# A planner that counts the port pair of VectorE and GpSimd as a resource, in a kernel of attention and two feed-forward networks

## Chip, cores and metric

One NeuronCore of a Trainium2 chip runs the kernel; the other cores are idle. The metric is the device time of one execution in microseconds (us). The engines are TensorE (PE in the profile's rows), VectorE (DVE), ScalarE (ACT), GpSimd (POOL) and SyncE (SP), which here issues all transfers.

## What is computed

Sliding-window attention with a distance bias, for 4 batches, 8 heads, 576 positions and head dimension 64, then a network with a softmax-weighted activation and layer norm, then a gated one, all in float32:

```python
scores = scale * np.matmul(q, k.transpose(0, 1, 3, 2))
mask = (rel >= 0) & (rel < 128)
scores = np.where(mask, scores + bias[None], -1000000000.0)
attn = np.exp(scores - np.max(scores, axis=-1, keepdims=True))
attn = attn / (np.sum(attn, axis=-1, keepdims=True) + 1e-09)
x = np.matmul(attn, v)                          # then (2304, 512)

h = x @ w_in                                    # (2304, 1024)
e = np.exp(h - np.max(h, axis=-1, keepdims=True))
solu = h * e / (np.sum(e, axis=-1, keepdims=True) + 1e-09)
mu = np.mean(solu, axis=-1, keepdims=True)
var = np.mean((solu - mu) ** 2, axis=-1, keepdims=True)
x = (solu - mu) / np.sqrt(var + 1e-06) * g_ln @ w_out

g = x @ w_gate                                  # (2304, 1536)
out = g * (1.0 / (1.0 + np.exp(-g))) * (x @ w_val) @ w_out
```

The weights arrive as 64-bit floats.

## The kernel before

**Numbers in two halves.** A float32 matrix product is made of three products of a faster type (fp32r): high by low, low by high, high by high. So each operand of the two networks exists as a high half (a cast, helper `high`, L201) and a low half (a subtraction, helper `low`, L205). `decode` (L213) turns one block of 128x512 weights into such halves: a transfer of 512 KB (tile dw), one square on ScalarE (L225), five operations on VectorE over tiles da and db (L230 to L238), an addition on GpSimd or VectorE (L241, L242), for w_out a scaling (L245), then `high` and `low`. There are 8 blocks of w_in, 8 of w_out and 36 of the second network's weights. Tiles dw, da and db have two buffers each.

**Stages.** Attention runs over 20 steps (4 batches by 5 query tiles of up to 128 rows), each of four pairs of heads, 80 units in all. `score` multiplies for two pairs at a time, one PSUM bank for each pair (L339). `attend` does the rest of a unit: for each head one VectorE operation that adds the bias and takes the maximum, out of PSUM (L372), and one exponential on ScalarE with the sum of the row as accumulator output (L375); then a sum of 1e-9 and a reciprocal over the two heads' sums (L381, L382), the normalization on GpSimd, ScalarE or VectorE (L387, L389), the transposition on TensorE (L409), a copy out of PSUM (L413 to L418) and the product with the values (L441). Results become xs, the halves of the first network's input. `up` makes a tile of 128 rows of it: two banks of 512 columns (L523), their maxima (L547, L554), exponentials (L557), products (L559), a squared deviation (L565), some one-column statistics (L561 to L574), a power on GpSimd (L579) and the normalization (L581, L582). `flip` transposes (L605), `down1` multiplies by w_out, and the result goes through DRAM (yscr). The second network, `gate_val` and `down`, takes the w2 blocks two chunks at a time, in six passes over all rows. Its first weights are decoded into the memory that attention leaves.

**Eight PSUM banks** (`bank_s`) serve the scores, transposes, values, halves of `up`, `flip` and `down1`. A unit returns its scores bank after the second L372.

**The order** is made by a planner in Python, class `Emitter`. Each stage is a generator that asks for slots (buffers) and hands in operations: an engine, a cost in ns, a function, and what it depends on. An operation may have several ways, one for each engine that can do it. `Emitter.run` takes for each operation the way with the least start + cost + handicap (`BIAS`: 1600 for VectorE, 700 for ScalarE), then the engine whose operation can start first, then the lowest rank; it calls the function, which writes the instruction, and sets the engine's busy time on by the cost. The rank goes by the row tile that the work belongs to. On the chip each engine runs its instructions in the order written, and waits only for data and buffers. So the costs decide who does what and in which order, and nothing of their times is enforced.

## Time and profile before

| what | us |
|---|---|
| median of 3 runs | 885.85 (885.5 to 887.36) |
| the profiled execution | 887.44, of which 885.7 are its span |
| TensorE busy (matmul) | 825.1, 93% of the span |
| VectorE busy | 492.9, 56% |
| ScalarE busy | 372.8, 42% |
| GpSimd busy | 317.0, 36% |
| mean granted clock of TensorE | 0.973 |

One execution was profiled; all rows come from it, with times in us from its first instruction. A busy share over the whole span is a mean over stages that differ, so the rows further down go by stretches: up to 132 us the weights of the first network are decoded beside the first attention steps, until 350 us attention and the first network run together, until 440 us the second network's first weights are decoded, and from then on it runs.

### The profile page before, as it was taken

The page shows a single profiled execution, that of the slowest core. Times are in us where ns is not written, and L with a number is a line of the kernel's source. Part 1 is how long each engine was busy: PE and PEld are TensorE (multiplying, and loading weights), DVE is VectorE, ACT ScalarE, POOL GpSimd, SP SyncE. Part 2 cuts the span into 40 slices and gives each one's busy share as a digit, 9 for nine tenths or more (in the row PEclk, how much of TensorE's full clock was granted, in tenths as well). Part 3 has the DMA queues.
Part 4 walks back from the last instruction along what each step waited for, and adds up shares of the span by engine and source line. Part 5 has one row for each costly group of instructions (what it writes and reads, how often), then busy time and mean ns, then how long its engine had stood idle before and what let it go on. Part 6 is the DMA issues. An engine that isn't in the chain of part 4 may idle for free.

```text
span 885.7 us, 13165 instructions
## 1 busy us (share of the span) xinstructions
PE 825.1 (93%) x4968; PEld 677.9 (77%) x4968; DVE 492.9 (56%) x1188; ACT 372.8 (42%) x948; POOL 317.0 (36%) x274
## 2 busy tenths in 40 slices
PE   5769879999999999968799999999999999999997
PEld 3547658788888888968588888887887887888885
DVE  5988993654556445888510186258337526822222
ACT  4667885864766656444432322122122213211110
POOL 2464661322123121665731154145216414521111
PEclk9779899999999999979999999999999999999999
DMA  7543311311121102333320022012003101100112
GB/s 253 168 138 105 96 60 44 107 37 54 50 72 49 36 8 97 119 104 112 120 94 1 1 72 72 1 49 72 24 0 86 58 1 48 47 1 13 60 57 85
DMA packets 23776, 59.12 MB, mean 67 GB/s; under 512 B 2592, under 2 KB 5280, under 8 KB 23712
## 3 DMA queue, kind: packets, MB, share of 16 engines
q1 hardware_dynamic: 23712, 58.28, 20.3%
q8 instruction: 39, 0.64, 0.3%
q14 instruction: 25, 0.20, 0.1%
HBM read 48.83 MB, written 9.44 MB: 66 GB/s over the span
## 4 chain that ended last, share of the span: by engine, by line
PE 70%; DVE 17%; POOL 4%; issue 4%; ACT 4%; DMA 1%; SPq 0%; POOLq 0%; ACTq 0%; DVEq 0%
PE gv L523 28%; PE bank L523 16%; PE o L523 15%; PE bank L441 3%; PE bank L409 3%; PE bank L339 3%; DVE db L234 2%; DVE da L230 2%; DVE da L238 2%; DVE da L236 2%; POOL db L241 2%; DVE e L372 2%; DVE db L232 1%; PE bank L605 1%; ACT e L375 1%
## 5 line engine op out<-in xcount | busy, mean ns | idle before, releaser
L523 PE MATMUL gv<-y,w 128*128 128x512 f32 (+1 forms) x1392 | 316.2, 378 | 3.1 <-POOL y L208 3.1
L523 PEld LDWEIGHTS gv<-y,w 128*128 128x128 f32 x1392 | 249.0, 189 | 57.6 <-POOL y L208 3.5
L523 PE MATMUL o<-w,a 128*128 128x512 f32 x648 | 170.0, 398 | 5.2 <-ACT ys L202 2.2
L208 POOL TENSOR_TENSOR a<-sg,a 128x512 fp32r<-128x512 f32 (+1 forms) x60 | 73.9, 1232 | 237.7 <-ACT a L202 237.2
L523 PEld LDWEIGHTS o<-w,a 128*128 128x128 f32 x648 | 121.1, 190 | 34.6 <-POOL a L208 3.8
L795 DVE TENSOR_TENSOR acc<-acc,o 128x512 f32<-128x512 f32 x90 | 61.2, 684 | 119.9 <-PE o L523 119.8
L523 PE MATMUL bank<-lnT,wout 128*128 128x256 f32 x864 | 116.9, 287 | 3.0 <-ACT lnT L202 2.5
L523 PEld LDWEIGHTS bank<-lnT,wout 128*128 128x128 f32 x864 | 109.0, 191 | 8.6 <-ACT lnT L202 2.7
L523 PE MATMUL bank<-win,xs 128*128 128x512 f32 x432 | 114.9, 404 | 0.1
L202 ACT CAST a<-sg 128x512 fp32r<-128x512 f32 (+1 forms) x59 | 34.0, 577 | 181.8 <-DVE sg L769 181.8
L769 DVE TENSOR_TENSOR sg<-sg,gv 128x512 f32<-128x512 f32 (+1 forms) x58 | 37.1, 639 | 126.7 <-PE gv L523 97.2
L241 POOL TENSOR_TENSOR db<-db,da 128x512 f32<-128x512 f32 x51 | 72.0, 1413 | 96.5 <-DVE da L238 93.9
L523 PEld LDWEIGHTS bank<-win,xs 128*128 128x128 f32 x432 | 76.5, 189 | 17.1 <-issue 2.1
L389 POOL TENSOR_TENSOR e<-e,st 128x512 f32<-128x512 f32 (+2 forms) x55 | 52.2, 948 | 103.9 <-DVE st L382 41.6
L375 ACT ACTIVATE e<-e,st 128x256 f32<-128x256 f32 (+2 forms) x160 | 75.0, 471 | 28.9 <-DVE st L372 28.8
L409 PE MATMUL bank<-ident,e 128*128 128x128 f32 (+2 forms) x288 | 47.7, 292 | 24.3 <-POOL e L389 15.0
L372 DVE CUSTOM_DVE_ANT_0 e<-bank,bias 128x256 f32<-128x256 f32 (+2 forms) x160 | 54.3, 376 | 17.2 <-PE bank L339 11.7
L409 PEld LDWEIGHTS bank<-ident,e 128*128 128x128 f32 (+2 forms) x288 | 31.4, 147 | 36.3 <-POOL e L389 18.2
L441 PE MATMUL bank<-pt,v 128*64 128x128 f32 (+2 forms) x576 | 51.4, 292 | 6.2 <-ACT pt L415 5.3
L230 DVE SCALAR_TENSOR_TENSOR da<-db,dw 128x512 f32<-128x512 f32 x52 | 46.6, 897 | 18.5 <-ACT db L225 18.4
L767 ACT ACTIVATE sg<-gv 128x512 f32<-128x512 f32 (+1 forms) x58 | 32.3, 557 | 56.3 <-PE gv L523 43.5
L202 ACT CAST w<-db 128x512 fp32r<-128x512 f32 x35 | 21.7, 621 | 80.1 <-POOL db L241 80.0
(70 smaller groups left out, 906.3 us busy)
## 6 DMA issues: line engine op xcount, KB each, us to landing
dw<-w SPq DMA_DIRECT2D x36, 512.0 KB, 3.6
raw<-qk SPq DMA_DIRECT2D x38, 256.0 KB, 3.7
yscr<-ys SPq DMA_DIRECT2D x9, 512.0 KB, 2.9
ysg<-yscr SPq DMA_DIRECT2D x9, 512.0 KB, 3.3
out<-acc SPq DMA_DIRECT2D x18, 256.0 KB, 2.0
v<-v SPq DMA_DIRECT2D x16, 256.0 KB, 2.8
dw<-w_in SPq DMA_DIRECT2D x8, 512.0 KB, 4.0
dw<-w_out SPq DMA_DIRECT2D x8, 512.0 KB, 3.5
```

The costliest lines, as they stand in the source:

```text
L202: return [(ACT, t_act(n, sbuf), lambda: nc.scalar.copy(hi, src)), (DVE, t_dve(n, sbuf), lambda: nc.vector.tensor_copy(hi, src))]
L208: ways.append((POOL, t_pool(n), lambda: nc.gpsimd.tensor_sub(lo, src, hi.bitcast(F32))))
L230: x = yield (DVE, t_dve(512), lambda: nc.vector.scalar_tensor_tensor(af, bf, MIN_HIGH * MIN_HIGH, hf, ALU.is_ge, ALU.mult), [x])
L241: x = yield ([(POOL, t_pool(512), lambda: nc.gpsimd.tensor_add(bf, bf, af)), (DVE, t_dve(512), lambda: nc.vector.tensor_add(bf, bf, af))], ...
L372: d = yield (DVE, t_dve(cols), lambda j=j: nc.vector.tensor_tensor_reduce(e[0:n, j, 0:cols], sc[0:n, j * 256:j * 256 + cols], bias[0:n, 2 ...
L375: ex.append((yield (ACT, t_act(cols, True, True), lambda j=j: nc.scalar.activation(e[0:n, j, 0:cols], e[0:n, j, 0:cols], AF.Exp, bias=st[0 ...
L389: eng.tensor_tensor(e[0:n, :, 0:cols], e[0:n, :, 0:cols], st[0:n, 6:8].unsqueeze(2).to_broadcast([n, 2, cols]), ALU.mult)
L409: nc.tensor.transpose(tp[0:kp, kb, j, 0:n], e[0:n, j, x * P:x * P + kp], ident[0:n, 0:n])
L441: nc.tensor.matmul(px[j * 64:(j + 1) * 64, pr, 0:n], vt[c - 1 + kb][0:kp, h * 64:(h + 1) * 64], pt[0:kp, kb, j, 0:n], start=(kb == 1), sto ...
L523: nc.tensor.matmul(o, terms[m][0], terms[m][1], start=(m == 0), stop=(m == len(terms) - 1))
L769: x = yield (DVE, t_dve(n), lambda: nc.vector.tensor_mul(sg, sg, gv[1][0]), [x, gv[1][1]])
L795: y = yield (DVE, t_dve(512), lambda o=o, tt=tt: nc.vector.tensor_add(acc[tt], acc[tt], o), [x])
```

## The change

`Emitter` gets a third kind of busy time, "+". Engine names that end in "+" can start only when the engine and "+" are free, and set both. All of GpSimd's operations have it (`POOL` is now "POOL+"), and of VectorE's those that read SBUF alone: the five of `decode`, the addition and scaling, `high` and `low` from SBUF, and the normalizations. VectorE's operations that read PSUM, and those on one or two columns, don't.

In `attend`, the exponentials' sums go to columns 0 and 1 of the unit's own scores bank in place of the tile st in SBUF, both L372 are handed in before both exponentials, and the bank is returned after L381 and L382. In `up`, L554, L571 and L574 take their one-column operands as pointer scalars of a `tensor_scalar`. Several costs change: matmul pieces from 216 to 233 or 231 ns for each matmul of 512 columns (109 to 120 and 0.4219 n to 0.457 n for the others), statistics of one column from 70 to 205 ns, the accumulating ScalarE operations by 93 ns, L381 and L382 from 230 to 360, L581 from 456 to 334. The handicaps and ranks stay.

```diff
+    def free(self, engine):
+        at = self.busy.get(engine.rstrip("+"), 0.0)
+        return max(at, self.busy.get("+", 0.0)) if engine.endswith("+") else at
+
     def run(self):
...
             for op in self.pending:
-                t, way = min(((max(self.busy.get(w[0], 0.0), op[2]), w) for w in op[3]), key=lambda x: x[0] + x[1][1] + BIAS.get(x[1][0], 0.0))
-                best.setdefault(way[0], []).append((t, op[0], op[1], op, way))
+                t, way = min(((max(self.free(w[0]), op[2]), w) for w in op[3]),
+                             key=lambda x: x[0] + x[1][1] + BIAS.get(x[1][0].rstrip("+"), 0.0))
+                best.setdefault(way[0].rstrip("+"), []).append((t, op[0], op[1], op, way))
             first = min(min(x[0] for x in ops) for ops in best.values())
...
             fn()
-            self.busy[engine] = t + cost
+            self.busy[engine.rstrip("+")] = t + cost
+            if engine.endswith("+"):
+                self.busy["+"] = t + cost
             op[5].settle(t + cost + self.HOP + op[4])
...
     em = Emitter()
-    PE, DVE, ACT, POOL, DMA = "PE", "DVE", "ACT", "POOL", "DMA"
+    PE, DVE, ACT, POOL, DMA = "PE", "DVE", "ACT", "POOL+", "DMA"
+    DVEP, NONE = "DVE+", "POOL"
     yscr = nc.dram_tensor("yscr", [NT // 256, P, KM, 256], F32).ap()
...
         return [(ACT, t_act(n, sbuf), lambda: nc.scalar.copy(hi, src)),
-                (DVE, t_dve(n, sbuf), lambda: nc.vector.tensor_copy(hi, src))]
+                (DVEP if sbuf else DVE, t_dve(n, sbuf), lambda: nc.vector.tensor_copy(hi, src))]
 
     def low(lo, src, hi, n, sbuf=True):
-        ways = [(DVE, t_dve(n), lambda: nc.vector.tensor_sub(lo, src, hi.bitcast(F32)))]
+        ways = [(DVEP if sbuf else DVE, t_dve(n), lambda: nc.vector.tensor_sub(lo, src, hi.bitcast(F32)))]
         if sbuf:
...
         af = a.bitcast(F32)
-        x = yield (DVE, t_dve(512), lambda: nc.vector.scalar_tensor_tensor(
+        x = yield (DVEP, t_dve(512), lambda: nc.vector.scalar_tensor_tensor(
             af, bf, MIN_HIGH * MIN_HIGH, hf, ALU.is_ge, ALU.mult), [x])
-        x = yield (DVE, t_dve(512, True), lambda: nc.vector.tensor_scalar(
+        x = yield (DVEP, t_dve(512, True), lambda: nc.vector.tensor_scalar(
             b, a, 3, 0x3FFFFFF8, ALU.logical_shift_left, ALU.bitwise_and), [x])
-        x = yield (DVE, t_dve(512), lambda: nc.vector.scalar_tensor_tensor(
+        x = yield (DVEP, t_dve(512), lambda: nc.vector.scalar_tensor_tensor(
             b, a, 0xC0000000, b, ALU.bitwise_and, ALU.bitwise_or), [x])
-        x = yield (DVE, t_dve(512, True), lambda: nc.vector.tensor_scalar(
+        x = yield (DVEP, t_dve(512, True), lambda: nc.vector.tensor_scalar(
             a, b, 0xFF800000, None, ALU.bitwise_and), [x])
-        x = yield (DVE, t_dve(512), lambda: nc.vector.scalar_tensor_tensor(
+        x = yield (DVEP, t_dve(512), lambda: nc.vector.scalar_tensor_tensor(
             af, lw, 2.0 ** -52, af, ALU.mult, ALU.mult), [x])
...
         x = yield ([(POOL, t_pool(512), lambda: nc.gpsimd.tensor_add(bf, bf, af)),
-                    (DVE, t_dve(512), lambda: nc.vector.tensor_add(bf, bf, af))], [x])
+                    (DVEP, t_dve(512), lambda: nc.vector.tensor_add(bf, bf, af))], [x])
         em.give(da_s, x)
...
             x = yield ([(ACT, 93 + t_act(512), lambda: nc.scalar.activation(bf, bf, AF.Copy, scale=scale)),
-                        (DVE, 456, lambda: nc.vector.tensor_scalar_mul(bf, bf, scale))], [x])
+                        (DVEP, 456, lambda: nc.vector.tensor_scalar_mul(bf, bf, scale))], [x])
         x = yield (high(hi, bf, 512), [x])
...
         bs_ok = bias_ok[0] if t == 0 and c == 0 else bias_ok[1]
-        ex = []
+        ex, ds = [], []
         for j in range(2):
...
                 -0.125, 3.0e38, ALU.add, ALU.min, st[0:n, j:j + 1]), [x, bs_ok])
-            ex.append((yield (ACT, t_act(cols, True, True), lambda j=j: nc.scalar.activation(
+            ds.append(d)
+        for j, d in enumerate(ds):
+            ex.append((yield (ACT, 93 + t_act(cols, True, True), lambda j=j: nc.scalar.activation(
                 e[0:n, j, 0:cols], e[0:n, j, 0:cols], AF.Exp, bias=st[0:n, j:j + 1], scale=-1.0,
-                accum_out=st[0:n, 2 + j:3 + j]), [d])))
-        em.give(bank_s, d, k)
+                accum_out=sc[0:n, j:j + 1]), [d, ds[0]])))
 
         def invert():
-            nc.vector.tensor_scalar_add(st[0:n, 4:6], st[0:n, 2:4], 1e-9)
+            nc.vector.tensor_scalar_add(st[0:n, 4:6], sc[0:n, 0:2], 1e-9)
             nc.vector.reciprocal(st[0:n, 6:8], st[0:n, 4:6])
...
 
-        x = yield (DVE, 230, invert, ex)
-        x = yield ([(DVE, t_dve(2 * cols), lambda: normalize(nc.vector)),
+        x = yield (DVE, 360, invert, ex)
+        em.give(bank_s, x, k)
+        x = yield ([(DVEP, t_dve(2 * cols), lambda: normalize(nc.vector)),
                     (ACT, 2 * (93 + t_act(cols)), lambda: normalize(nc.scalar)),
...
             terms = [(xs[a][:, k], win[c][:, k, cs]) for a, c in HALVES for k in range(KM)]
-            for p in pieces(h[q], terms, 6, 216.0):
+            for p in pieces(h[q], terms, 6, 233.0):
                 x = yield p
...
         es[i] = e
-        x = yield (DVE, 70, lambda: nc.vector.tensor_tensor(mx, mx, mx2, ALU.min), tops)
+        x = yield (DVE, 205, lambda: nc.vector.tensor_scalar(mx, mx, mx2, None, ALU.min), tops)
         us = []
         for q, (a, a2) in enumerate(((sm, su), (sm2, su2))):
-            y = yield (ACT, t_act(512, False, True), lambda q=q, a=a: nc.scalar.activation(
+            y = yield (ACT, 93 + t_act(512, False, True), lambda q=q, a=a: nc.scalar.activation(
                 e[:, q], h[q], AF.Exp, bias=mx, accum_out=a), [x])
...
                 e[:, q], h[q], 1.0, e[:, q], ALU.mult, ALU.mult, accum_out=a2), [y])))
-        x = yield (DVE, 70, lambda: nc.vector.tensor_scalar(
+        x = yield (DVE, 205, lambda: nc.vector.tensor_scalar(
             nmu32, su, su2, -1.0 / (32 * DF1), ALU.add, ALU.mult), us)
...
         for q, a in enumerate((va, va2)):
-            vs.append((yield (ACT, t_act(512, True, True), lambda q=q, a=a: nc.scalar.activation(
+            vs.append((yield (ACT, 93 + t_act(512, True, True), lambda q=q, a=a: nc.scalar.activation(
                 h[q], e[:, q], AF.Square, bias=nmu32, scale=1.0 / 32, accum_out=a), [x])))
...
             nc.vector.tensor_scalar(s1, sm, sm2, 1e-9, ALU.add, ALU.add)
-            nc.vector.scalar_tensor_tensor(eps, s1, 1e-6, s1, ALU.mult, ALU.mult)
-
-        y = yield (DVE, 280, moments, [x])
-        x = yield (DVE, 70, lambda: nc.vector.scalar_tensor_tensor(var, va, va2, eps, ALU.add, ALU.add), vs + [y])
+            nc.vector.tensor_scalar(eps, s1, 1e-6, s1, ALU.mult, ALU.mult)
+
+        y = yield (DVE, 615, moments, [x])
+        x = yield (DVE, 205, lambda: nc.vector.tensor_scalar(var, va, va2, eps, ALU.add, ALU.add), vs + [y])
         em.give(h_s, x)
...
         for q in range(2):
-            last = yield ([(DVE, 456, lambda q=q: nc.vector.tensor_scalar(
+            last = yield ([(DVEP, 334, lambda q=q: nc.vector.tensor_scalar(
                 e[:, q], e[:, q], nmu, rr, ALU.add, ALU.mult)), (POOL, 754, lambda q=q: nc.gpsimd.tensor_scalar(
...
             terms = [(wout[c][:, k, cs], ln[a][:, k]) for a, c in HALVES for k in range(KF1)]
-            for p in pieces(o[:, m % 2, :], terms, 12, 109.0):
+            for p in pieces(o[:, m % 2, :], terms, 12, 120.0):
                 x = yield p
...
             yield from decode(t[0][:, cs], t[1][:, cs], w2[c, :, cs])
-            x = yield (POOL, 0.0, lambda: None)
+            x = yield (NONE, 0.0, lambda: None)
             yield x
...
             terms = [(w[b][:, s * 512 + k * P:s * 512 + (k + 1) * P], y[a][:, k]) for a, b in HALVES for k in range(KM)]
-            for p in pieces(o, terms, 6, 0.4219 * n):
+            for p in pieces(o, terms, 6, 0.457 * n):
                 x = yield p
...
             terms = [(aT[c, g][a][:, cs], wc[c][b][:, 1024:1536]) for a, b in HALVES for c in cs2]
-            for p in pieces(o, terms, 3 * CPP, 216.0):
+            for p in pieces(o, terms, 3 * CPP, 231.0):
                 x = yield p
...
```

## Rows read from the trace of the kernel before

**Rows 1.** Busy time by stretch: PE, PEld, DVE, ACT, POOL, clock, DMA share, GB/s.

```profile
22.00:132.00 110.00, 84.96 (x596) 63.19 (x597) 104.74 (x297) 82.99 (x235) 59.89 (x53) 0.86 0.36 114
132.00:350.00 218.00, 216.59 (x1836) 182.21 (x1834) 114.54 (x469) 138.48 (x432) 54.80 (x67) 1.00 0.16 51
350.00:440.00 90.00, 73.45 (x482) 67.03 (x483) 70.89 (x113) 40.51 (x76) 54.99 (x38) 0.92 0.38 123
440.00:886.00 446.00, 438.96 (x1990) 357.75 (x1988) 190.18 (x269) 101.97 (x180) 141.73 (x108) 1.00 0.13 42
```

**Rows 2.** Chain of waits, 22 to 132 us, shares by line (the view cuts it).

```profile
by line: DVE da L230 11.1%; DVE e L372 10.7%; DVE db L234 9.7%; DVE da L238 7.8%; issue 6.8%; DVE db L232 5.0%; DVE da L236 5.0%; DVE st L381 4.8%; DVE mst L547 4.0%; DVE e L559 3.7%; ACT e L375 3.6%; DVE xs L206 3.1%; PE bank L409 2.9%; DV
```

**Rows 3.** TensorE's waits, 22 to 132 us: total us, times, longest.

```profile
PE bank L409 <- POOL e L389: 14.2, 6, 5.5
```

**Rows 4.** VectorE's operations, 22 to 132 us: busy us, mean ns, idle before.

```profile
L230 DVE SCALAR_TENSOR_TENSOR da<-db,dw 128x512 f32<-128x512 f32 x14 | 14.7, 1059 | 0.0
L234 DVE SCALAR_TENSOR_TENSOR db<-da,db 128x512 uint32<-128x512 uint32 x14 | 12.3, 878 | 0.0
L238 DVE SCALAR_TENSOR_TENSOR da<-dw,da 128x512 f32<-128x512 uint32 x14 | 11.0, 789 | 0.0
L381 DVE TENSOR_SCALAR st<-st 128x2 f32<-128x2 f32 (+1 forms) x26 | 9.5, 365 | 2.8 <-ACT e L375 2.7
L236 DVE TENSOR_SCALAR da<-db 128x512 uint32<-128x512 uint32 x14 | 7.8, 557 | 0.0
L232 DVE TENSOR_SCALAR db<-da 128x512 uint32<-128x512 uint32 x14 | 6.2, 448 | 0.0
...
L554 DVE TENSOR_TENSOR mst<-mst 128x1 f32<-128x1 f32 x5 | 3.3, 667 | 0.0
L206 DVE TENSOR_TENSOR win<-db,win 128x512 fp32r<-128x512 f32 x2 | 3.2, 1582 | 0.0
...
L571 DVE SCALAR_TENSOR_TENSOR mst<-mst 128x1 f32<-128x1 f32 x4 | 1.7, 436 | 0.1
...
L569 DVE TENSOR_SCALAR mst<-mst 128x1 f32<-128x1 f32 x4 | 0.8, 201 | 0.0
```

**Rows 5.** Timeline: start us, us, operation; GpSimd beside VectorE, then VectorE alone.

```profile
29.75 1.58 POOL L241 TENSOR_TENSOR db<-db,da 128x512 f32<-128x512 f32 x1 [2.57 <-DVE da L238]
...
30.13 1.22 DVE L381 TENSOR_SCALAR st<-st 128x2 f32<-128x2 f32 x1
...
113.98 1.22 POOL L582 TENSOR_SCALAR e<-e,mst 128x512 f32<-128x512 f32 x1
114.47 0.68 DVE L547 TENSOR_REDUCE mst<-bank 128x1 f32<-128x512 f32 x1
...
51.41 0.42 DVE L232 TENSOR_SCALAR db<-da 128x512 uint32<-128x512 uint32 x1
...
74.32 0.68 DVE L234 SCALAR_TENSOR_TENSOR db<-da,db 128x512 uint32<-128x512 uint32 x1
```

**Rows 6.** Timeline of VectorE: scores of 128 columns, and one unit's scores and sum.

```profile
80.45 0.28 DVE L372 CUSTOM_DVE_ANT_0 e<-bank,bias 128x128 f32<-128x128 f32 x1
...
113.17 0.42 DVE L372 CUSTOM_DVE_ANT_0 e<-bank,bias 128x256 f32<-128x256 f32 x1
...
119.64 0.16 DVE L381 TENSOR_SCALAR st<-st 128x2 f32<-128x2 f32 x1
```

**Rows 7.** ScalarE's operations, 22 to 132 us: busy us, mean ns, idle before.

```profile
L387 ACT ACTIVATE e<-e,st 128x256 f32<-128x256 f32 (+2 forms) x20 | 8.5, 475 | 5.0 <-DVE st L382 4.8
```

**Rows 8.** Chain of waits, 350 to 440 us, shares by line (the view cuts it).

```profile
by line: PE bank L523 19.9%; POOL db L241 11.1%; PE gv L523 11.1%; issue 8.7%; DMA dw<-w 8.2%; POOL w L208 6.1%; DVE da L230 4.4%; DVE db L234 4.1%; POOL y L208 3.7%; DVE da L236 3.6%; POOL e L582 3.4%; ACT w L202 2.8%; DVE lnT L206 2.7%; D
```

**Rows 9.** Low halves, 350 to 440 us: busy us, mean ns, idle before.

```profile
L206 DVE TENSOR_TENSOR w<-db,w 128x512 fp32r<-128x512 f32 x3 | 2.1, 687 | 0.0
...
L208 POOL TENSOR_TENSOR y<-ysg,y 128x1024 fp32r<-128x1024 f32 x5 | 12.9, 2586 | 10.8 <-ACT y L202 10.8
L208 POOL TENSOR_TENSOR w<-db,w 128x512 fp32r<-128x512 f32 x9 | 12.3, 1367 | 5.1 <-ACT w L202 5.1
```

## The prediction

> **What bounds the kernel now.** A mean over the whole span says little here, so the first view is the table by stretch [rows 1]. Over its four stretches TensorE works for 84.96+216.59+73.45+438.96 = 814 of 864 us. From 132 to 350 us and from 440 us on it is full, 216.59 of 218 us and 438.96 of 446, at a granted clock of 1.00, the upper of the two levels: whatever happens on the other engines can shorten these 664 us by no more than the 8.4 us that they leave. The other two stretches are different. From 22 to 132 us TensorE works for 84.96 of 110 us at a mean clock of 0.86, and VectorE for 104.74: VectorE is the full engine. From 350 to 440 us TensorE works for 73.45 of 90 us, VectorE for 70.89 and GpSimd for 54.99. So 25 + 16.5 us of idle TensorE time, and some clock, are what the change can win.
>
> The second view, the chain of waits of the first of these stretches, says the same: the VectorE parts that its line prints add up to 11.1+10.7+9.7+7.8+5.0+5.0+4.8+4.0+3.7+3.1 = 65% [rows 2]. The third, TensorE's own waits, has another name at its head: 14.2 us, in six waits, for GpSimd's normalized exponentials, L389 [rows 3]. I keep that for a rival.
>
> Why is VectorE full? In its table of operations [rows 4] many means are far over what the operation takes elsewhere, and the timeline shows why. L381, a sum over two columns, takes 1.22 us while a GpSimd addition of 1.58 us runs [rows 5], and 0.16 us at another place [rows 6]. L547, which reads PSUM, takes 0.68 us although L582 runs on GpSimd beside it [rows 5]. So for some forms, those that read SBUF tensors alone, the two engines exclude each other, and the loser waits for the whole operation of the other.
>
> **The change, part by part.**
>
> (a) The sums of exponentials go to the scores' own PSUM bank, so L381 reads PSUM. For its 26 instances at 365 ns [rows 4] I expect 185: between the 160 of a free instance [rows 6] and L569's 201 [rows 4]. An outer bound is 280, what L372 takes for 128 columns out of PSUM [rows 6]. Saved: 26 x 0.18 = 4.7 us of VectorE; with the bounds 2.2 to 5.3. [...]
>
> (b) L554, L571 and L574 become the form with pointer scalars, which L569 has now, at 201 ns [rows 4]. L554 stands five times at 667; L571 four times at 436, and L574 as often and much alike. Saved: 5 x 0.46 + 8 x 0.23 = 4.2 us. The bound on the other side is that the new forms are stopped like the old ones: 0.
>
> (c) The rule of choice: GpSimd's operations and VectorE's SBUF forms now share one more busy time. Each GpSimd operation raises it, so a VectorE SBUF form can never be planned earlier than the same step on GpSimd, and VectorE carries a handicap of 1600 ns. For the low halves of SBUF tensors (601+1600 against 1226; of 1024 columns 1135+1600 against 2303), the additions L241/L242 and the normalizations, GpSimd or ScalarE now always win. What VectorE still has of these goes. In this stretch that is three low halves of weights (two of win at 1582 ns [rows 4], one of wout alike) and one addition, L242, taken at the 0.68 us of an L234 that runs alone [rows 5]: 5.4 us off VectorE, and 4 x 1.3 = 5.2 us onto GpSimd, whose 59.89 busy us of 110 [rows 1] cover it as long as nobody waits for it. Normalizations may also move on to ScalarE, 2 x 475 ns each [rows 7]; with 27 us idle there [rows 1] it could hold all 16 of GpSimd's, 15 us, but only just.
>
> (d) The order. The five VectorE operations of a decoded block take 1059+448+878+557+789 = 3731 ns [rows 4]. With 0.68 us for the three of one kind and 0.42 for the two of the other, as where GpSimd is idle [rows 5], they would take 2.88. Over 14 blocks that is 11.9 us of waiting for GpSimd. If the plan comes true, work on PSUM stands beside GpSimd's and some of this goes; if not, the 5.2 us more of GpSimd work add 11.9 x 5.2/59.9 = 1.0 us. I take -2 out of +1.0 to -11.9, nearer the bad end: the queues of the two engines don't wait for each other's operations, so an order alone ties nothing down.
>
> Sum on VectorE for 22 to 132 us: 4.7+4.2+5.4+2.0 = 16.3 us; with its 65% of the chain, 10.6 us of the end.
>
> (e) What is added. The first exponential of a unit now overwrites a column of the scores and may have to wait for the second L372 too, 0.42 us [rows 6]; behind it in ScalarE's queue stand the casts and squares of the decoding, and VectorE and GpSimd wait for those. 26 units x 0.42 = 10.9 us of delay on an engine with 27 us idle: I put down +1.0, out of 0 to +3. A scores bank is kept until the sums are read: in one unit this goes from the end of its second L372 at 113.6 us to the end of L381 at 119.8 [rows 6], six us more. I put down +0.5 and price the bad case below.
>
> (f) 350 to 440 us. GpSimd has 11.1+6.1+3.7+3.4 = 24% of the chain [rows 8], 22 us of its 55 busy ones, so 0.4 of what it does is on the path; VectorE has 4.4+4.1+3.6+2.7 = 15%, 0.2 of its work. The rule of (c) gives GpSimd three low halves (w) at 1.37 us and one of 1024 columns (y) at 2.6 [rows 9]: 6.7 us. It takes 3 x 0.69 [rows 9] and twice that for the one of y off VectorE, and (b) another 6 x 0.23: 4.9 us. Net 6.7 x 0.4 - 4.9 x 0.2 = +1.7, from -4 (order helps here too) to +6.
>
> (g) The other edits, costs of matmul pieces by 7 to 10% and of a few statistics, change only the plan's clock. Where TensorE is full, the order of its pieces has no price beyond the 8.4 us: 0.
>
> Total: -10.6 + 1.0 + 0.5 + 1.7 = -7.4 us. The profiled execution took 887.44 us, 885.7 of it span; its share goes one for one against the median of the runs, 885.85: 878.5.
>
> **The rivals.**
>
> (1) The port order comes true in full. For: waiting for GpSimd is the largest thing that VectorE does not need. Against: no instruction enforces it. Price: another 9.9 x 0.65 = 6.4 us, and for 12 blocks in the other stretch, if they wait as long each, 12 x 0.85 x 0.2 = 2.0: 870. [...]
>
> (2) Slower, through the banks. Eight PSUM banks serve scores, transposes, values, the first network's halves and its flips. From 66 to 132 us some 12 units each keep theirs about 5 us longer (the row of (e) is one): 60 bank-us in 66 us, nearly one bank of eight. It decides where the other seven are taken: then each of six pairs of scores comes later by half a hold, 2.5 to 3 us, with it TensorE's attention and the network behind it, and 16 us come on top of -7.4: 894. Against: at the head of TensorE's waits stands L389, not a bank [rows 3].
>
> (3) GpSimd takes VectorE's place. TensorE's largest wait is for L389 [rows 3]. If half of what VectorE saves lies beside that wait and the 5.2 us more on GpSimd's queue reach TensorE in full, it is -5.3 + 5.2 + 1.5 + 1.7 = +3.1: 889.
>
> (4) The change doesn't do what it says: the order stays in effect as it was, and only (a) and (b) remain: 8.9 x 0.65 = 5.8 us, less 1.5 of (e): 881.5.
>
> **How the numbers follow.** Forecast 0.47 (own range 872 to 884); rival 1 0.18; rival 2 0.15; rival 3 0.12; rival 4 0.08. A measurement of this kernel can tell about 0.2%, 1.8 us, from no change. Faster: 0.47+0.18+0.08, less a tail of 0.03: 0.70. Same: 0.05, of that tail and of rival 3's lower part. Slower: rival 2 and the rest of rival 3: 0.25. The range goes from 864 to 891: it leaves out about half of rival 2 and holds the bounds of (d) and (f).
>
> **What would show it.** In the changed kernel's table, L381's line at about 185 ns and the three statistics at about 200, whatever runs beside them; no low half of an SBUF tensor on VectorE; VectorE's busy time up to 132 us down by some 16 us, and TensorE's full stretch starting some 8 us earlier. A decoded block well under 3.7 us on VectorE speaks for rival 1; a new wait of the scores, L339, for rival 2; a larger wait for L389 for rival 3. I am wrong if VectorE becomes emptier and the full stretch starts no earlier.

## The result, and the profile after

The changed kernel takes 863.21 us (median of 4 runs, 862.76 to 863.35) against 885.89 us before (4 runs, 885.5 to 887.36): 0.9745 of the time, with a 95% interval of 0.9732 to 0.9758. The forecast was 878.5 with a range of 864 to 891. The direction held; the gain is 22.7 us, three times the 7.4 forecast, and the time lies just below the range.

The stretch table of the changed kernel (columns as in [rows 1]; the last stretch ends with the span, 861.6 us):

```profile
22.00:132.00 110.00, 93.17 (x714) 67.86 (x715) 89.24 (x322) 92.95 (x275) 62.38 (x58) 0.92 0.36 120
132.00:350.00 218.00, 216.04 (x1778) 181.62 (x1777) 109.82 (x447) 132.59 (x402) 61.60 (x72) 1.00 0.18 59
350.00:440.00 90.00, 84.24 (x513) 74.35 (x512) 63.18 (x96) 44.58 (x81) 66.69 (x45) 0.98 0.36 120
440.00:862.00 422.00, 415.27 (x1895) 338.52 (x1893) 187.18 (x264) 94.78 (x169) 137.21 (x103) 1.00 0.12 40
```

Against [rows 1], TensorE does 8 us more work from 22 to 132 us, VectorE 15.5 us less and ScalarE 10 us more; from 350 to 440 us TensorE works for 84 us instead of 73. The two stretches that had room gave it, and nothing was lost in the full ones. Of the 24.1 us by which the span is shorter (885.7 to 861.6), 4.9 are TensorE's own busy time, 825.1 to 820.1 us for the same 4968 matmuls while its mean granted clock goes from 0.973 to 0.988 (both traces show two levels of it, 1.00 and 0.50); the other 19.2 are time in which it stood idle.

To say where the time went, two events are better than fixed windows, since the work moves against the clock: the last product of attention with the values (L441 before, L452 after) and the first product of the second network into tile gv, which comes when its first group is through. Rows by tile, TensorE: count, duration, first and last start. Before:

```profile
L441 PE MATMUL bank<-pt,v x576: 218/273/477, 11.3 to 350.3; 128*64 128x128 f32 x152, 64*64 64x64 f32 x20, 128*64 128x64 f32 x20
L523 PE MATMUL gv<-y,w x1392: 277/396/629, 426.0 to 872.2; 128*128 128x512 f32 x164, 128*128 128x256 f32 x35
```

After:

```profile
L452 PE MATMUL bank<-pt,v x576: 218/273/477, 11.6 to 339.6; 128*64 128x128 f32 x152, 64*64 64x64 f32 x20, 128*64 128x64 f32 x20
L534 PE MATMUL gv<-y,w x1392: 277/395/652, 405.1 to 849.5; 128*128 128x512 f32 x164, 128*128 128x256 f32 x35
```

Attention ends at 339.6 instead of 350.3 us (-10.7). From there to gv it takes 65.5 instead of 75.7 us (-10.2), and from gv to the end of the span 456.5 instead of 459.7 (-3.2). So the gain has two halves of equal size. The first was forecast at -9.1 (10.6 less the 1.5 of (e)), the second at +1.7. I call the three parts attention, turn and rest below.

The VectorE table of the changed kernel, 22 to 132 us (busy us, mean ns, idle before it):

```profile
L239 DVE SCALAR_TENSOR_TENSOR da<-db,dw 128x512 f32<-128x512 f32 x14 | 10.8, 780 | 1.9 <-ACT db L234 1.9
L247 DVE SCALAR_TENSOR_TENSOR da<-dw,da 128x512 f32<-128x512 uint32 x12 | 9.2, 775 | 0.0
L243 DVE SCALAR_TENSOR_TENSOR db<-da,db 128x512 uint32<-128x512 uint32 x13 | 8.7, 682 | 0.0
...
L241 DVE TENSOR_SCALAR db<-da 128x512 uint32<-128x512 uint32 x13 | 6.2, 491 | 0.0
L245 DVE TENSOR_SCALAR da<-db 128x512 uint32<-128x512 uint32 x12 | 5.2, 444 | 0.0
...
L391 DVE TENSOR_SCALAR st<-bank 128x2 f32<-128x2 f32 (+1 forms) x31 | 4.7, 151 | 3.3 <-ACT e L386 3.2
...
L585 DVE TENSOR_SCALAR mst<-mst 128x1 f32<-128x1 f32 x5 | 1.3, 270 | 0.3 <-ACT bank L576 0.2
L565 DVE TENSOR_SCALAR mst<-mst 128x1 f32<-128x1 f32 x6 | 1.2, 206 | 0.1
L582 DVE TENSOR_SCALAR mst<-mst 128x1 f32<-128x1 f32 x5 | 1.1, 215 | 0.2
```

A decoded block now takes 780+491+682+444+775 = 3172 ns where it took 3731 [rows 4]; the sum over two columns (now L391) 151 instead of 365; the three statistics (now L565, L582, L585) 206 to 270 instead of 436 to 667. No low half of an SBUF tensor is left on VectorE. VectorE is idle for 20.8 of the 110 us, where it was for 5.3 (110 less the busy times of the two stretch tables). Its place among TensorE's waits of 22 to 132 us has gone to ScalarE's normalizations (L397):

```profile
PE bank L420 <- ACT e L397: 10.9, 7, 6.1
PE bank L452 <- ACT pt L426: 2.3, 3, 1.1
...
PE bank L420 <- POOL e L399: 0.7, 1, 0.7
```

The 14.2 us for GpSimd's normalizations [rows 3] have shrunk to 0.7, and ScalarE's, 1.9 us in the kernel before, are now the largest:

```profile
PE bank L409 <- ACT e L387: 1.9, 2, 1.7
```

### The profile page after: what moved, and what is told of

It reads as the page before. It is cut to its first block, busy times and chain, and to the rows that moved or that the text cites. A ratio compares the mean times of both kernels' runs of the same rounds, so it can differ in the third digit from the quotient of the medians.

```text
span 861.6 us, 13190 instructions
## 1 busy us (share of the span) xinstructions
PE 820.1 (95%) x4968; PEld 670.2 (78%) x4968; DVE 460.5 (53%) x1173; ACT 373.7 (43%) x951; POOL 333.0 (39%) x286
## 4 chain that ended last, share of the span: by engine, by line
PE 75%; DVE 10%; ACT 6%; POOL 4%; issue 3%; DMA 1%; SPq 0%; POOLq 0%; ACTq 0%; DVEq 0%
PE gv L534 29%; PE bank L534 20%; PE o L534 15%; PE bank L452 4%; PE bank L420 3%; PE bank L348 3%; DVE db L243 2%; ACT e L386 2%; PE bank L616 1%; DVE da L247 1%; POOL a L217 1%; DVE da L239 1%; DVE da L245 1%; DVE lnT L215 1%; ACT e L397 1%
## 5 line engine op out<-in xcount | busy, mean ns | idle before, releaser
L217 POOL TENSOR_TENSOR a<-sg,a 128x512 fp32r<-128x512 f32 (+1 forms) x60 | 77.7, 1295 | 222.1 <-ACT a L211 222.1
L534 PE MATMUL bank<-win,xs 128*128 128x512 f32 x432 | 118.2, 411 | 1.0 <-ACT bank L576 0.9
L399 POOL TENSOR_TENSOR e<-e,st 128x512 f32<-128x512 f32 (+2 forms) x55 | 50.4, 918 | 132.4 <-DVE st L392 47.1
L381 DVE CUSTOM_DVE_ANT_0 e<-bank,bias 128x256 f32<-128x256 f32 (+2 forms) x160 | 53.9, 377 | 20.4 <-PE bank L348 12.4
L239 DVE SCALAR_TENSOR_TENSOR da<-db,dw 128x512 f32<-128x512 f32 x52 | 47.9, 924 | 30.4 <-ACT db L234 30.2
L217 POOL TENSOR_TENSOR w<-db,w 128x512 fp32r<-128x512 f32 x36 | 51.0, 1418 | 17.5 <-ACT w L211 17.5
L452 PE MATMUL bank<-pt,v 128*64 128x128 f32 (+2 forms) x576 | 50.0, 286 | 5.1 <-ACT pt L426 2.3
```

The costliest lines, as they stand in the source:

```text
L217: ways.append((POOL, t_pool(n), lambda: nc.gpsimd.tensor_sub(lo, src, hi.bitcast(F32))))
L239: x = yield (DVEP, t_dve(512), lambda: nc.vector.scalar_tensor_tensor(af, bf, MIN_HIGH * MIN_HIGH, hf, ALU.is_ge, ALU.mult), [x])
L381: d = yield (DVE, t_dve(cols), lambda j=j: nc.vector.tensor_tensor_reduce(e[0:n, j, 0:cols], sc[0:n, j * 256:j * 256 + cols], bias[0:n, 2 ...
L399: eng.tensor_tensor(e[0:n, :, 0:cols], e[0:n, :, 0:cols], st[0:n, 6:8].unsqueeze(2).to_broadcast([n, 2, cols]), ALU.mult)
L452: nc.tensor.matmul(px[j * 64:(j + 1) * 64, pr, 0:n], vt[c - 1 + kb][0:kp, h * 64:(h + 1) * 64], pt[0:kp, kb, j, 0:n], start=(kb == 1), sto ...
L534: nc.tensor.matmul(o, terms[m][0], terms[m][1], start=(m == 0), stop=(m == len(terms) - 1))
```

## Experiments

Four parts of the change can be made alone: **ab**, the sums in PSUM and the pointer scalars with their costs; **c**, the shared busy time in the planner; **d**, TensorE's costs in the planner. All ratios are against runs of the kernel before on the same chip, beside the kernel in question.

### e6_before_hop and e7_after_hop: how much is chance

An order that a planner makes moves in many places for any change of a cost. Edit of both, once on the kernel before and once on the changed one:

```diff
-    HOP = 90.0
+    HOP = 91.0
```

> The kernel before with 91 ns instead of 90 between an operation and those that depend on it, in the planner alone: the order changes in many places for no reason. It gives the size of chance: both theories expect 882 to 889. A larger shift would mean that differences of that size between orders tell nothing of a cause.

> The changed kernel with 91 ns instead of 90 between an operation and those that depend on it, in the planner alone: the size of chance on this side. 860 to 867; a larger shift would mean that the changed kernel's order was a lucky one.

Measured: 886.88 us, 1.0028 (1.0017 to 1.0039), and 862.37 us, 0.9749 (0.9733 to 0.9765). Though matmuls, casts and decode steps change places, each kernel keeps its time within 0.3%. Two reshufflings are few, but they say that differences of 1% below are hardly luck, and that a difference of 0.3% between two orders may be.

### e1_bcode: pointer scalars alone, in the old order

```diff
-nc.vector.tensor_tensor(mx, mx, mx2, ALU.min)
+nc.vector.tensor_scalar(mx, mx, mx2, None, ALU.min)
-nc.vector.scalar_tensor_tensor(eps, s1, 1e-6, s1, ALU.mult, ALU.mult)
+nc.vector.tensor_scalar(eps, s1, 1e-6, s1, ALU.mult, ALU.mult)
-nc.vector.scalar_tensor_tensor(var, va, va2, eps, ALU.add, ALU.add)
+nc.vector.tensor_scalar(var, va, va2, eps, ALU.add, ALU.add)
```

> The kernel before with the three one-column statistics L554, L571 and L574 in the form with pointer scalars, at the planner's old costs, so that every engine keeps its order. By the port reading the three take about 205 ns wherever they stand: up to 132 us 4.2 us less VectorE time, of which 65% on the path, so 883 us (-2.7); from 350 to 440 us at most another 0.5. If the new forms are stopped by GpSimd like the old ones, or if what VectorE saves is hidden, it stays at 885.9.

Measured: 883.47 us, 0.9985 (0.9973 to 0.9996). Attention ends 1.3 us earlier (349.0). The order is the same here, so this is a small gain of the kind forecast, half its size.

### e8_ab, e2_plus, e3_pecost: each part alone

e8_ab has the edits of `attend` and `up` (and the costs of those operations), e2_plus those of `Emitter` and of the engine names, with L581's cost of 334, e3_pecost these:

```diff
-            for p in pieces(h[q], terms, 6, 216.0):
+            for p in pieces(h[q], terms, 6, 233.0):
...
-            for p in pieces(o[:, m % 2, :], terms, 12, 109.0):
+            for p in pieces(o[:, m % 2, :], terms, 12, 120.0):
...
-            for p in pieces(o, terms, 6, 0.4219 * n):
+            for p in pieces(o, terms, 6, 0.457 * n):
...
-            for p in pieces(o, terms, 3 * CPP, 216.0):
+            for p in pieces(o, terms, 3 * CPP, 231.0):
```

> The kernel before with sums in PSUM, pointer scalars and the costs of both, without the shared busy time and with TensorE's old costs. By the prediction's steps (a), (b) and (e), -5.8 + 1.5: 881 to 882. If shorter VectorE operations are worth something only in an order that knows of the port: 885 to 890.

> The kernel before with the shared busy time of GpSimd and VectorE's SBUF forms in the planner alone (and L581's cost of 334); instructions, sums, statistics and TensorE costs as before. Theory P (the shared port in the plan is what the change is worth, by the order and by the truer clock of the decoding): attention ends 6 to 8 us earlier and the second network's first group 10 us earlier still, 868 to 872. Theory C (the plan's TensorE costs put the first pieces of the second network at their place): only the first stretch gains, 876 to 880.

> The kernel before with the four TensorE costs of the planner alone (233, 120, 0.457 n, 231). Theory C: the stretch from 350 to 440 us gains about 10 us, 874 to 877, and attention ends where it did. Theory P: within 3 us of 885.9, either way, by chance of order.

Measured: e8_ab 886.08 us, 1.0014 (1.0004 to 1.0024); e2_plus 873.27 us, 0.9876 (0.9861 to 0.9892); e3_pecost 896.13 us, 1.0136 (1.0119 to 1.0153).

So the shorter VectorE operations alone bring nothing, the shared busy time alone brings 11 us, and truer TensorE costs alone cost 12. (e8_ab also has the new costs of the shortened operations, so its order is not quite the old one.) In e8_ab VectorE is emptier from 22 to 132 us, 97.62 us for the 104.74 of [rows 1]; its stretch row (columns as in [rows 1]) and TensorE's waits there:

```profile
22.00:132.00 110.00, 86.39 (x620) 65.27 (x620) 97.62 (x298) 83.90 (x241) 66.37 (x57) 0.85 0.33 113
...
PE bank L412 <- ACT e L389: 8.8, 2, 5.3
PE bank L412 <- POOL e L391: 6.1, 4, 3.2
```

Attention ends at 348.4 us, 1.9 earlier. TensorE gains 1.4 us of work in the stretch; it waits for normalizations as before, now for ScalarE's more than for GpSimd's. That VectorE was 95% busy and held 65% of the chain did not mean that time taken off it comes back. Part of it did not even stay off VectorE. The five operations of a decoded block, 22 to 132 us, in e8_ab:

```profile
L231 DVE SCALAR_TENSOR_TENSOR da<-db,dw 128x512 f32<-128x512 f32 x14 | 13.7, 980 | 1.9 <-ACT db L226 1.8
L235 DVE SCALAR_TENSOR_TENSOR db<-da,db 128x512 uint32<-128x512 uint32 x14 | 12.9, 921 | 0.0
L239 DVE SCALAR_TENSOR_TENSOR da<-dw,da 128x512 f32<-128x512 uint32 x14 | 11.7, 834 | 0.0
L237 DVE TENSOR_SCALAR da<-db 128x512 uint32<-128x512 uint32 x14 | 8.8, 630 | 0.0
L233 DVE TENSOR_SCALAR db<-da 128x512 uint32<-128x512 uint32 x14 | 8.5, 608 | 0.2
```

That is 980+608+921+630+834 = 3973 ns for a block, 242 more than before [rows 4]: 3.4 us over 14 blocks. Some of the waiting for GpSimd that the sums and statistics lost has come back in the decoding.

In e3_pecost attention ends where it did (350.2 us), the turn takes 80.0 instead of 75.7 us and the rest 463.9 instead of 459.7. In the rest one wait has spread; TensorE's waits from 440 us on, in it:

```profile
PE o L523 <- POOL a L208: 6.1, 8, 1.1
```

The kernel before has 1.7 us of the same in 4 waits. The products o now stand too early in TensorE's queue for their input a. A likely reason, not tested, is that the old costs of TensorE, 7 to 10% below the new ones, had made up for what the plan did not know of the other engines.

### e4_noplus, e5_nopecost, e13_cd: one part left out

The changed kernel without c, without d, and without ab.

> The changed kernel without the shared busy time: sums in PSUM, pointer scalars, all new costs. Theory P: the 5.8 us of the shorter VectorE operations, less some delay of the exponentials, 879 to 882. Theory C: those and the 10 us of the later stretch, 868 to 872.

> The changed kernel with the old TensorE costs in the planner. Theory S (the shared busy time, sums in PSUM and pointer scalars carry the gain; TensorE's costs only hurt or do nothing): 858 to 866. Theory T (the costs of the engines must be true together; with the shared port known, TensorE's true costs help): 868 to 875.

> The kernel before with the shared busy time and the new TensorE costs, without sums in PSUM and pointer scalars. If TensorE's costs help as soon as the port is known to the plan: 866 to 870. If they help only together with operations that really run beside GpSimd: 873 or more.

Measured: 894.33 us, 1.0115 (1.0091 to 1.0138); 869.4 us, 0.9835 (0.9811 to 0.9859); 881.61 us, 0.9964 (0.9954 to 0.9974). With e8_ab, e2_plus and e3_pecost this completes the table, each entry (ratio - 1) x 885.4 us:

| | old TensorE costs | new TensorE costs (d) |
|---|---|---|
| old planner, old instructions | 0 | +12.0 |
| old planner, ab | +1.2 | +10.2 |
| shared busy time (c), old instructions | -11.0 | -3.2 |
| shared busy time (c), ab | -14.6 | -22.6 |

The parts don't add. ab is worth +1.2 alone, -3.6 beside c and -19.4 beside c and d; d costs 8 to 12 us everywhere but in the last row, where it brings 8. Only c works by itself. The 7.8 us that d costs beside c alone are lost in attention, which ends at 351.8 us in e13_cd and at 345.5 in e2_plus.

### e11_poolonly and e10_slowdecode: is it the choice, the clock, or the order?

The shared busy time does three things at once: it takes low halves, additions and normalizations off VectorE, it makes the decoding take longer in the plan, and it lays GpSimd's operations beside VectorE's work on PSUM. e11_poolonly does the first alone, by leaving VectorE out of the ways:

```diff
-        ways = [(DVE, t_dve(n), lambda: nc.vector.tensor_sub(lo, src, hi.bitcast(F32)))]
         if sbuf:
-            ways.append((POOL, t_pool(n), lambda: nc.gpsimd.tensor_sub(lo, src, hi.bitcast(F32))))
+            ways = [(POOL, t_pool(n), lambda: nc.gpsimd.tensor_sub(lo, src, hi.bitcast(F32)))]
```

(and the same for L242, L389 and L581). e10_slowdecode does the second alone; its first line, the others alike:

```diff
-        x = yield (DVE, t_dve(512), lambda: nc.vector.scalar_tensor_tensor(
+        x = yield (DVE, 897, lambda: nc.vector.scalar_tensor_tensor(
             af, bf, MIN_HIGH * MIN_HIGH, hf, ALU.is_ge, ALU.mult), [x])
```

> The kernel before with the VectorE ways of low halves of SBUF tensors, the decoding's addition and the normalizations taken out, so that the choice of engine is that of the shared busy time and nothing else of it. By step (c) of the prediction 5.4 us less VectorE time up to 132 us give 3.5 us, less some in the later stretch: 882 to 884. Theory P (order, not choice): 884 to 889. Should it come to 875, choice is all that the shared busy time does.

> The kernel before with the decoding's costs in the planner set to what its trace shows, 897, 547, 1033, 702 and 807 ns for the five VectorE operations and 1413 for GpSimd's addition; no shared busy time. Theory R (the gain comes from a truer clock of the decoding in the plan): most of the shared busy time's 11 us, 873 to 878. Theory P (it comes from keeping GpSimd and VectorE's SBUF forms apart): chance alone, 883 to 889.

Measured: 889.34 us, 1.0053 (1.0038 to 1.0068), and 886.63 us, 1.002 (1.001 to 1.0029). The choice alone brings nothing; its loss of 4.7 us, not far above the 2.5 of e6_before_hop, lies in the turn (attention ends at 350.1, gv begins at 429.5). The truer clock splits: the turn takes 66.1 us instead of 75.7, as in the changed kernel, but attention ends at 356.0, 5.7 us later. So in the turn, time for the decoding in the plan is most of what the shared busy time gives; in attention it is not, and what is left to help there is the order. The traces bear that out: from 22 to 132 us a decoded block takes 3078 to 3358 ns in the eight kernels that have c there, and 3474 to 4050 ns in the ten that do not.

### e12_sbufsum and e14_oldstats: the changed order with the old instructions

Costs and planner stay as in the changed kernel, so every engine keeps its order; e12_sbufsum puts the sums into SBUF, e14_oldstats undoes the edits of e1_bcode:

```diff
-                accum_out=sc[0:n, j:j + 1]), [d, ds[0]])))
+                accum_out=st[0:n, 2 + j:3 + j]), [d, ds[0]])))
...
-            nc.vector.tensor_scalar_add(st[0:n, 4:6], sc[0:n, 0:2], 1e-9)
+            nc.vector.tensor_scalar_add(st[0:n, 4:6], st[0:n, 2:4], 1e-9)
```

> The changed kernel, every engine in its order, but with the exponentials' sums in SBUF again, so that L391 reads SBUF and is stopped by GpSimd. Theory F (the PSUM sums make true what the plan takes for granted, that this operation runs beside GpSimd): L391 back to 300 ns or more, 4 us and more of VectorE time up to 132 us, 866 to 869. If VectorE is not on the path there any more: 863 to 865, or less, since the first exponential then waits less.

> The changed kernel, every engine in its order, with the three statistics in their old form, which reads two SBUF columns. If they meet GpSimd as often as in the kernel before: 4 us of VectorE time up to 132 us, 865 to 868. If the order keeps them apart or VectorE is not on the path: 863 to 864.

Measured: 871.73 us, 0.986 (0.9813 to 0.9908), with runs from 868.12 to 876.78, and 866.69 us, 0.979 (0.9762 to 0.9817). The line of the sum in e12_sbufsum, 22 to 132 us (its profile is of the slowest of the four runs):

```profile
L391 DVE TENSOR_SCALAR st<-st 128x2 f32<-128x2 f32 (+1 forms) x28 | 14.4, 515 | 1.4 <-ACT e L386 1.4
```

515 ns, against 151 in the changed kernel and 365 before [rows 4]. In this order the sum loses more to GpSimd than it did in the old one, because the planner puts it there, as an operation that GpSimd does not stop. The same happens in e2_plus, where the planner already counts the sum as one that GpSimd does not stop, and it is stopped (its table, 22 to 132 us):

```profile
L389 DVE TENSOR_SCALAR st<-st 128x2 f32<-128x2 f32 (+1 forms) x26 | 13.6, 522 | 2.6 <-ACT e L383 2.6
```

So the PSUM sums are worth some 8.5 us and the pointer scalars 3.5 us in the new order (differences of medians; by single runs 5 to 14 and 0 to 5), against 1.3 us for the pointer scalars in the old order and nothing for both together in e8_ab. They make true what the plan takes for granted. A small part of the 8.5 may be ScalarE's, whose accumulator reads are 33 ns longer in e12_sbufsum (last section); that was not separated.

### e15_lateplus: the shared busy time in the later stretch alone

On the kernel before, with the planner's edits, counted from the moment at which attention's memory is given back:

```diff
-        return max(at, self.busy.get("+", 0.0)) if engine.endswith("+") else at
+        return max(at, self.busy.get("+", 0.0)) if self.late and engine.endswith("+") else at
...
         esa.close()
+        em.late = True
```

> The kernel before, with the shared busy time counted by the planner only once attention is planned to its end. Attention must end where it did, at 350 us. If the later stretch's gain is the work of the shared busy time there: its first two chunks end 6 to 8 us earlier, 877 to 880. If it was an echo of the earlier stretch: 884 to 890.

Measured: 877.59 us, 0.9917 (0.9901 to 0.9933). The two events in it:

```profile
L450 PE MATMUL bank<-pt,v x576: 218/273/476, 11.6 to 350.5; 128*64 128x128 f32 x152, 64*64 64x64 f32 x20, 128*64 128x64 f32 x20
...
L532 PE MATMUL gv<-y,w x1392: 277/395/796, 414.5 to 863.8; 128*128 128x512 f32 x164, 128*128 128x256 f32 x35
```

Attention ends where it did, the turn takes 64.0 us instead of 75.7, and some of that goes again in the rest (461.3 instead of 459.7). The second half of the gain is the shared busy time at work in the turn, no echo of the first.

### e9_w2late: what does TensorE stand still for in the turn?

In the kernel before, TensorE's longest wait of the turn is one of 8.4 us for w. Timeline of the kernel before (start us, us, operation, in brackets the idle time before it):

```profile
376.78 1.04 PE L605 MATMUL bank<-ident,e 128*128 128x128 f32 x8
...
379.71 1.69 POOL L241 TENSOR_TENSOR db<-db,da 128x512 f32<-128x512 f32 x1
...
381.43 0.62 ACT L202 CAST w<-db 128x512 fp32r<-128x512 f32 x1 [4.40 <-POOL db L241]
381.96 1.07 ACT L202 CAST lnT<-bank 128x512 fp32r<-128x512 f32 x2
...
386.18 2.08 PE L523 MATMUL bank<-y,w 128*128 128x256 f32 x8 [8.36 <-POOL w L208]
```

The first reading was that TensorE's queue has the products with w too far ahead. The test moves just those:

```diff
-            w2_ok[c][j].settle(x.time)
+            w2_ok[c][j].settle(x.time + (8000.0 if c < CPP else 0.0))
```

> The kernel before, with the second network's first six blocks of weights taken for ready 8 us later by the planner alone; no engine's work changes, only the place of a few matmuls in TensorE's queue. Theory Q (in the later stretch TensorE stands still because its first products with w are queued ahead of finished work, not because weights come late): the wait of 8.4 us for w goes and the end comes 6 to 9 us earlier, 877 to 880. If the weights' decoding itself sets the end: 885 to 888.

Measured: 889.26 us, 1.0049 (1.0032 to 1.0065). That theory fell. TensorE's waits in it, 350 to 440 us:

```profile
PE bank L523 <- ACT lnT L202: 13.6, 2, 8.7
```

The wait for w is gone and one for lnT is in its place, to nearly the same moment (387.3 us instead of 386.2). The rows above show what it stands behind: the last flips (376.78) are done, so the casts of lnT could run, but ScalarE has a cast of w ahead of them that waits 4.40 us for GpSimd's addition. Moving this one piece of TensorE's order did not help. ScalarE's waits of this kind, 350 to 440 us before and 340 to 430 us after:

```profile
ACT w L202 <- POOL db L241: 18.5, 10, 4.4
```

```profile
ACT w L211 <- POOL db L250: 8.7, 8, 2.4
```

They are halved, which fits e10_slowdecode, where they are 12.3 us from 356.3 to 441.8 us. That the casts are the link was not tested by itself, and another explanation fits all runs better: less decoding stands ahead of gv. One of the five VectorE operations of a decoded block, counted from attention's end to gv's first product, before, after and in e10_slowdecode:

```profile
L234 DVE SCALAR_TENSOR_TENSOR db<-da,db 128x512 uint32<-128x512 uint32 x12 | 10.7, 895 | 0.2
```

```profile
L243 DVE SCALAR_TENSOR_TENSOR db<-da,db 128x512 uint32<-128x512 uint32 x10 | 12.0, 1198 | 0.1
```

```profile
L234 DVE SCALAR_TENSOR_TENSOR db<-da,db 128x512 uint32<-128x512 uint32 x10 | 9.7, 966 | 0.2
```

All five together are 60 operations, 12 blocks, in the kernel before, 48 in the changed one and 49 in e10_slowdecode. It is so in every kernel: the eight whose turn takes 75 to 80 us all run 60 of them before gv begins, and the ten whose turn takes 64 to 68 us, the nine with c and e10_slowdecode, run 44 to 50. Nor is the decoding itself faster: 65.5 us after attention's end, 51 of these operations have started in the kernel before and 48 in the changed one. So a plan in which the decoding takes longer lets gv begin ahead of the last blocks, which belong to the next pass, and it is in just these kernels that the turn is shorter. Which queue holds gv back in the old order was not tested.

### e16_bact1000: is ScalarE the next bound?

```diff
-B_ACT = 700.0
+B_ACT = 1000.0
```

> The changed kernel with ScalarE's handicap in the planner at 1000 instead of 700 ns, so that more normalizations go to GpSimd. If ScalarE, busy for 93 of 110 us there, holds attention now (TensorE waits 10.9 us for its normalizations): 856 to 861. If GpSimd and the port are as scarce: 863 to 870.

Measured: 865.08 us, 0.9781 (0.9761 to 0.98), no faster than the changed kernel. ScalarE does 40 operations of normalization instead of 50, GpSimd 60 instead of 55, and TensorE still waits 14.8 us for ScalarE's from 22 to 132 us. Moving normalizations back to GpSimd brings nothing, so ScalarE is not a bound that yields to this. No version tried beats the changed kernel by more than chance.

## Why the prediction was wrong

By parts of the span: attention -10.7 us where -9.1 was forecast, the turn -10.2 where +1.7 was, the rest -3.2 where 0 was. So the step that put the time out is (f), which priced the turn by what GpSimd and VectorE have on the chain and gave the order there no number. The first part came near by luck, as its terms show.

**Attention: the sum nearly right, its terms not.** Term by term on VectorE, 22 to 132 us: (a) 4.7 forecast, 26 x (365-151) = 5.6 measured. (b) 4.2 forecast, 5 x (667-206) + 4 x (436-215) + 4 x (450-270) = 3.9 measured. (c) 5.4 forecast, and all the operations did go; one of them, L242, had taken 0.97 us and not the 0.68 put down, so 5.7. (d) was the mis-sized term: I took 2 of 11.9 us, with the argument that an order ties nothing down; 14 blocks at 3172 instead of 3731 ns give 7.8. The order did most of what rival 1 said, though no instruction enforces it. Why it holds on the chip was not tested; the engines wait for each other's data all the time (in the changed kernel GpSimd's additions alone 30.2 us for the decoding on VectorE, 22 to 132 us), which may keep them near the plan. By the prediction's own rule the measured terms, 5.6+3.9+5.7+7.8 = 23.0 us, would have given 0.65 x 23.0 - 1.5 = 13.4 us instead of the 10.7: a term too small and a rule too generous partly cancelled.

What carried the first half was not the sum, however. Were the terms independent, (a) and (b) alone would have given 5.8 us less the 1.5 of (e); e8_ab came out 1.2 us slower. Were (c) a gain, e11_poolonly would have shown one; it lost 4.7 us. And in the new order (a) is worth 8.5 us, not 3 (e12_sbufsum). The step that failed here is the factor of the sum: VectorE is full and has 65% of the chain, so 65% of what comes off it was taken off the end [rows 1, 2]. The chain names what was last in one order. When VectorE gets faster and the planner does not know of the exclusion, normalizations on ScalarE and GpSimd are what TensorE waits for, 14.9 us in e8_ab, and other VectorE operations take over part of the waiting for GpSimd. This was rival 3's point, and I gave it the wrong trigger.

**The turn: wrong in sign.** Step (f) had +1.7 us, from 6.7 us more on a GpSimd that holds 24% of the chain [rows 8]. By itself that fits: e11_poolonly, which has the choice alone, is 3.7 us slower in the turn (79.4 against 75.7 us). But the shared busy time as a whole was worth -11.7 there (e15_lateplus), and (f) gave the order no number but a bound of -4. What it left out is that the order decides how much decoding stands ahead of gv: 60 VectorE operations before, 48 after.

**Step (g)**, which put the other edits at 0 because they change only the plan's clock, was wrong both ways: +12.0 us alone, -8.0 in the company of the rest (e3_pecost, e5_nopecost). The full stretches can give no more than the 8.4 us that they leave, but an order can also make them less full, as e3_pecost shows: 6.1 us of waits for a from 440 us on instead of 1.7.

**(e)** The waits of the exponentials and the longer held banks, the core of rival 2, did not show as waits. From 22 to 132 us the exponentials wait 0.5 us for the operation out of the scores (L381, before L372), where it was 3.7; and the only waits of the scores' matmuls (L348, before L339) in the whole run are 6.8 us for a transfer, as before. A later place in the plan would not show as a wait, so (e)'s 1.5 us are not measured. With chances, rival 1 (870) was the nearest; its price was too small because it had the first half's order and almost nothing for the second.

## What to carry to other kernels

When an order is written by a planner, its costs and resources are one model, and a correction has to be judged with the others: here truer TensorE costs made things slower in three settings out of four, and paid only where the plan knew of the shared resource and the instructions behaved as the plan says. When two engines exclude each other, as these two do here (a sum that takes 141 ns at the least took up to 1224), give operations a form that the other engine does not stop, and let the planner put them beside it: here the forms alone were worth nothing, the planner alone 11.0 us, and both with the new costs 22.6. And a full engine's share of the chain says what was last in one order, not what a change of the order gives: look for what is queued next behind it, and for work of a later stage that stands ahead of an earlier one's.

## What the runs showed of the hardware

The form decided. A sum over two columns takes 139 to 163 ns in all 80 instances when it reads PSUM, though 53 of them run beside a GpSimd operation, and 141 to 1224 when it reads SBUF. The rows by line, after and before:

```profile
L391 DVE TENSOR_SCALAR st<-bank x80: 139/155/163, 7.7 to 331.5; 128x2 f32<-128x2 f32 x64, 64x2 f32<-64x2 f32 x16
```

```profile
L381 DVE TENSOR_SCALAR st<-st x80: 141/169/1224, 7.6 to 344.8; 128x2 f32<-128x2 f32 x64, 64x2 f32<-64x2 f32 x16
```

At two columns PSUM thus costs nothing extra (shortest 139 and 141 ns, medians 155 and 169). Of the 80 that read SBUF 24 take over 200 ns, and each of these ends 21 to 48 ns after a GpSimd operation does. GpSimd is stopped too: in the kernel before, its addition L241 takes 1403 to 1724 ns in the 20 instances that begin during one of the five VectorE operations of a decoded block, and 1263 to 1304 in the 18 that begin during one that reads PSUM. What the title and the expectations call a port shows in the traces as these times alone; its mechanism no run shows. The one-column statistics with pointer scalars take 206 and 214 ns with one such operand and 270 with two over the whole run, and never more than 216 and 276, though all their operands lie in SBUF and 22 of the 54 run beside a GpSimd operation; so it is not all forms that read SBUF alone which GpSimd stops, as the prediction had it. Their old forms are shorter when nothing stops them (medians 149, 159 and 218 ns) and take up to 1267. Unexpected, and small: ScalarE's read of its accumulator became shorter when it writes to PSUM. The rows of the exponentials' reads by form, after and before:

```profile
L386 ACT ACTIVATION_READ_ACCUMULATOR e<-e,st 128x1 f32 x128 | 20.2, 158 | 0.0
```

```profile
L375 ACT ACTIVATION_READ_ACCUMULATOR e<-e,st 128x1 f32 x128 | 24.4, 191 | 0.0
```

In e12_sbufsum, with the same order and the sums in SBUF, it is 191 ns again. In the changed kernel the first network's reads, which still write to SBUF, take 202 (L568) and 189 ns (L576). 33 ns on each of 160 reads are 5 us of ScalarE over the run, in a kernel where ScalarE is now 93 of 110 us busy in the attention stretch.

The new TensorE costs are the truer ones: in the kernel before, at the clock's 1.00, six fp32r matmuls of 512 columns (L523, bank<-win,xs) take 1.39 us from 301.04 us on, 232 ns each, which the plan had at 216 and has at 233. That is 0.45 ns for a column; four float32 matmuls of 128 columns (L441, eight records) take 0.59 us from 305.70 us on, 1.15 ns for a column.
